# Rebuilding the first two batches of a fused attention and MLP kernel: loads by head pairs, global columns by one-hot matmuls, weights and MLP placed earlier

## The chip, the cores and the metric

The kernel runs on one core of one Trainium2 chip. The metric is the device time of one execution in microseconds (us); lower is better. A kernel's executions differ by about 1% among themselves, so a difference below about half a per cent is not a difference here.

The engines, as the profile names them: PE does matmuls (PEld its weight loads), DVE, ACT and POOL do elementwise work, SP issues DMAs. POOL and ACT issue DMAs too. SPq is SP's queue of issues. PEclk is the clock granted to PE, as a share of full speed.

## The reference, cut to what matters

Eight batches, eight heads, 576 tokens, head size 64 (model width 512). Attention sees a band of 32 tokens to either side and eight global tokens, which see and are seen by all. Then comes a ResMLP block: a mix over tokens, and an MLP over channels of width 2048.

```python
mask = np.abs(pos[:, None] - pos[None, :]) <= window            # 32
mask = mask | is_global[:, None] | is_global[None, :]
attn = softmax(where(mask, scale * q @ k.T, -1e9))
x = (attn @ v)                                                  # [8, 576, 512]
a1 = alpha1 * x + beta1
u = x + lam * np.einsum('ts,bsd->btd', w_tok, a1)               # token mixing
a2 = alpha2 * u + beta2
out = u + lam * (np.maximum(a2 @ w_ch1, 0.0) @ w_ch2)           # MLP
```

## The kernel before

The program is written as one order of instructions; each engine works off its own part of it in that order. Tokens of all batches are lined up and cut into nine groups of 512 for the MLP. Each group needs 64 matmuls with W1 and 64 with W2, 128x128 by 128x512, 1152 in all. They are the bulk of the work, and they are used as fill: the front of a batch (attention and token mixing) is a generator that yields how many MLP matmuls of earlier groups to put in.

```python
def filler():
    for g in range(9):
        while g >= done[0]:
            yield False
        yield from mlp(g)
fill = filler()
for _ in range(8):
    next(fill)
for b in range(1, NB):
    gen = front(b, kqn)
    ...                                  # for each n that gen yields: n times next(fill)
```

Within the front, batch b + 1 is prepared: K and Q arrive in five chunks, which POOL casts (`qk_chunk`), and which a transposing DMA then turns. Three small gathers fetch the K, Q and V rows of the global tokens. POOL also forms XL, the scaled attention output, from which token mixing reads. The V shift makes a second copy of V, offset by 64 tokens, with two DMAs. UT is the MLP's input, transposed.

```python
def front(b, kqn):
    x = pX.tile([P, 5, DM], FP32, name="x")
    if not last:
        cq = [qk_chunk(b + 1, c) for c in range(3)]      # loads on SP; casts later on POOL (G)
        kq, vg = gathers(b + 1)                          # three indirect DMAs on POOL
    yield from pg(b)
    yield from qk(b, 0)
    for c in range(2):
        if cq: cq.pop(0)(G)
    for p in range(4):                                   # head pairs
        ...                                              # scores of pair p + 1
        pv(b, p, x)                                      # P @ V, x on DVE, XL on POOL
        if not last:
            if p == 0:
                cq.pop(0)(G)
                cq = [qk_chunk(b + 1, c) for c in (3, 4)]
            elif p == 1:
                cq.pop(0)(G); cq.pop(0)(G)
            elif p == 2: ...                             # transposing DMAs of K and Q, loads of V
            else: ...                                    # casts of V, V shift, global V
        yield 2
    yield 22
    mix = tokmix(b, x)
    ...
```

The first two batches are written out by hand. In batch 0 all K and Q are loaded first, in halves of four heads. Batch 1's K and Q are loaded early, and cast and transposed between the steps of batch 0's attention and token mixing. Then V of batch 1, then W2:

```python
pv(0, 1, x)
drain(qk3)
xg(0, 2)
wt_tr(1)
kt(0, (SC, SC))                  # batch 1's K, pair 0: PE transposes, ACT copies
n_q0(SC)                         # batch 1's first Q half: cast on ACT
pv(0, 2, x)
w1_dma(0)
...
c_v = [v_part(1, i) for i in range(3)]
for c in c_v:
    c(G)                         # batch 1's V: casts on POOL
v_shift(G)
for blk in range(4):
    w2_dma(blk)                  # W2, four loads of 512 KB, issued by POOL
```

The softmax here doesn't subtract the row's maximum and nothing guards it: scores larger than these inputs give would overflow.

Of the kernel before, what the change touches and what calls it, by code (L numbers as in the profile page):

```python
# [20 lines left out]
D = 64  # L21
# [15 lines left out]
def _consts():  # L37
    p = np.arange(P)[:, None]
    t = np.arange(NSUB)[None, :]
    key = 64 * t - 32 + p  # L40
    q = np.arange(64)[None, :]
    band = ((p - q >= 0) & (p - q <= 2 * WIN)).astype(np.float32)
    valid = ((key >= 0) & (key < S)).astype(np.float32)
    h = (np.arange(P) % 64) // 8
    par = (h[:, None] % 2 == np.arange(2)[None, :]).astype(np.float32)
    bd = (h[:, None] == np.arange(8)[None, :]).astype(np.float32)
    oh = (np.arange(P)[:, None] % 8 == np.arange(8)[None, :]).astype(np.float32)
    hoff = ((h * S)[:, None] + np.arange(8)[None, :] * H * S).astype(np.float32)
    return np.concatenate([key.astype(np.float32), valid, band, par, bd, oh, hoff], axis=1).astype(np.float32)


C_KEY, C_VALID, C_BAND, C_PAR, C_BD, C_OH, C_HOFF = 0, 9, 18, 82, 84, 92, 100
C_W = 108
# [3 lines left out]
def kernel(  # L57
# [89 lines left out]
    b2a = cp.tile([P, 4], BF16, name="b2a")  # L147

    wt16 = A(HTb, 0, [[704, 5], [1, 704]])
    KQ0 = 3520  # L150
# [10 lines left out]
    def qk4_half(b, i, hh, r):  # L161
        nc.sync.dma_start(
            out=A(r, 0, [[256, 4], [1, 256]]),
            in_=(k, q)[i][b, 4 * hh : 4 * hh + 4, 0:512, :].rearrange("h (p c) d -> p h (c d)", c=4),
        )
        return lambda E: copy(E, out=A(HTb, KQ0 + 2560 * i + 256 * hh, [[64, 4], [512, 4], [1, D]]), in_=A(r, 0, [[256, 4], [64, 4], [1, D]]))

    def qk4_rest(b, r):
        for i, src in enumerate((k, q)):
            nc.sync.dma_start(out=A(r, 0, [[64, 8], [1, 64]], 64 * i, 64), in_=src[b, :, 512:576, :].rearrange("h p d -> p h d"))  # L170
        return lambda E: copy(E, out=A(HTb, KQ0 + 2048, [[1, 512]]), in_=r[:, 0:512])
# [34 lines left out]

    def v_shift(E):
        E.dma_start(out=A(vo, 0, [[1, 2080]], 0, 64), in_=A(ve, 0, [[1, 2080]], 64, 64))
        E.dma_start(out=A(vo, 0, [[1, 2080]], 64, 64), in_=A(ve, 520, [[1, 2080]], 0, 64))

    def gathers(b):
        kq = pS.tile([P, D], FP32, name="kq")
        vg = pS.tile([64, D], FP32, name="vg")
# [3 lines left out]
        G.indirect_dma_start(out=vg, out_offset=None, in_=vf, in_offset=off)  # L217
        return kq, vg
# [115 lines left out]
    def pv(b, p, x):  # L334
        par = b % 2
        ptz, gs, rs, xl = PTz[p % 2], GS[par], RS[par], XL[par]
        xps = psX.tile([P, 2, 512], FP32, name="xps")
        for hh in range(2):
            h = 2 * p + hh
            for u in range(5):  # L340
                o_ = xps[:, hh, 65 * u : 65 * u + 65]
# [6 lines left out]
                T.matmul(out=o_, lhsT=gs[:, P * u : P * u + P], rhs=rs[:, h, :], start=False, stop=True)  # L348
        rden = pS.tile([P, 2, 5], FP32, name="rden")
        V.tensor_scalar(out=rden, in0=A(xps, 64, [[512, 2], [65, 5]]), scalar1=EPS, scalar2=None, op0=ALU.add)  # L350
        V.reciprocal(out=rden, in_=rden)
        V.tensor_tensor(  # L352
            out=A(x, P * p, [[64, 2], [DM, 5], [1, 64]]),
            in0=A(xps, 0, [[512, 2], [65, 5], [1, 64]]),
            in1=A(rden, 0, [[5, 2], [1, 5], [0, 64]]),
            op=ALU.mult,
        )
        full, edge, r0 = (0, 4, 0) if par == 0 else (1, 0, 64)
        G.tensor_tensor(  # L359
# [5 lines left out]
        G.tensor_tensor(  # L365
# [43 lines left out]
    def front(b, kqn):  # L409
# [3 lines left out]
        if not last:  # L413
            cq = [qk_chunk(b + 1, c) for c in range(3)]
            kq, vg = gathers(b + 1)
# [5 lines left out]
        for p in range(4):  # L421
# [11 lines left out]
            if not last:  # L433
                if p == 0:
                    cq.pop(0)(G)
                    cq = [qk_chunk(b + 1, c) for c in (3, 4)]
                elif p == 1:
                    cq.pop(0)(G)
                    cq.pop(0)(G)
                elif p == 2:  # L440
# [5 lines left out]
                else:  # L446
# [5 lines left out]
        yield 22  # L452
# [46 lines left out]
    nc.sync.dma_start(out=gi_t, in_=bass.AP(gi32.tensor, gi32.offset, [[0, P], [1, 16]]))  # L499
    nc.sync.dma_start(out=cst, in_=nc.inline_tensor(_consts(), name="cst_np").ap())  # L500
    scr, a1b, b1r, colr = u_tile(), u_tile(), u_tile(), u_tile()
    stage = [pUT.tile([P, 1024], FP32, name="UT") for _ in range(2)]
    c_k0 = qk4_half(0, 0, 0, next_r())
    c_q0 = qk4_half(0, 1, 0, next_r())
    c_rest = qk4_rest(0, stage[1])
    c_k1 = qk4_half(0, 0, 1, next_r())
    c_q1 = qk4_half(0, 1, 1, stage[0])

    make_identity(nc, identb)
    G.memset(dum, 0.0)  # L510
    SC.activation(out=dum, in_=dum, func=AF.Exp)
    G.memset(RV[0][0:32, 0:512], 0.0)
    G.iota(colr, pattern=[[1, DM]], base=0, channel_multiplier=0, allow_small_or_imprecise_dtypes=True)
    G.memset(GS[0], 0.0)
    G.memset(RS[0], 0.0)
    G.memset(A(PTz[1], 0, [[128, 19], [1, 64]]), 0.0)

    V.memset(KTz, 0.0)
    V.memset(KgT, 0.0)
    V.memset(A(QT, 1664, [[80, 16], [1, 8]]), 0.0)  # L520
    V.memset(A(ve, 64, [[65, 40], [1, 1]]), 1.0)
    for t_ in GRT:
        V.memset(t_, 0.0)
    SC.copy(out=A(kz, 64, [[256, 20], [64, 2], [1, 64]]), in_=A(KTz, 0, [[128, 20], [64, 2], [1, 64]]))
    SC.copy(out=A(PTz[0], 0, [[128, 19], [1, 64]]), in_=A(KTz, 0, [[64, 19], [1, 64]]))
    V.tensor_copy(out=gbc, in_=A(gi_t, 0, [[2, 8]]))
    V.tensor_tensor(out=scr[:, 0:8], in0=gbc, in1=cst[:, C_OH : C_OH + 8], op=ALU.mult)
    V.tensor_reduce(out=gsel[:, 0:1], in_=scr[:, 0:8], axis=mybir.AxisListType.X, op=ALU.add)
    V.tensor_tensor(out=hg_idx, in0=cst[0:64, C_HOFF : C_HOFF + 8], in1=A(gsel, 0, [[0, 8]], 0, 64), op=ALU.add)
    kq, vg = gathers(0)  # L530
    masks_a(scr)

    def kt(p, engs):
        ps = ml(BF16)
        for c in range(4):
            T.transpose(out=ps[:, c * P : (c + 1) * P], in_=A(HTb, KQ0 + 512 * c + P * p, [[1, P]]), identity=identb)
        for hh in range(2):
            copy(engs[hh], out=A(KTz, 640 * (2 * p + hh) + 32, [[4, P], [1, 4]], 64 * hh, 64), in_=A(ps, 0, [[1, P], [P, 4]], 64 * hh, 64))

    def qt(p):  # L540
        ps = sc(BF16)
        for c in range(4):
            T.transpose(out=ps[:, c * P : (c + 1) * P], in_=A(HTb, KQ0 + 2560 + 512 * c + P * p, [[1, P]]), identity=identb)
        for e in range(2):
            SC.copy(out=A(QT, 1600 * e + 80 * p, [[320, 4], [4, 16], [1, 4]]), in_=A(ps, 16 * e, [[32, 4], [1, 16], [P, 4]]))  # L545

    def rest():
        ps = ml(BF16)
        for p in range(4):
            T.transpose(out=ps[:, P * p : P * p + P], in_=A(HTb, KQ0 + 2048 + P * p, [[1, P]]), identity=identb)  # L550
        for hh in range(2):
            V.tensor_copy(out=A(KTz, 640 * hh + 544, [[1280, 4], [1, 64]], 64 * hh, 64), in_=A(ps, 0, [[P, 4], [1, 64]], 64 * hh, 64))
        SC.copy(out=A(QT, qo(8), [[80, 4], [1, 64]]), in_=A(ps, 64, [[P, 4], [1, 64]]))

    c_k0(V)
    c_v = [v_part(0, i) for i in range(3)]
    nc.sync.dma_start(out=a1b, in_=moe_alpha1.unsqueeze(0).to_broadcast([P, DM]))
    nc.sync.dma_start(out=lamb, in_=moe_lam.unsqueeze(0).to_broadcast([P, DM]))
    for r0 in (0, 64):
        nc.sync.dma_start(out=b1r[r0 : r0 + 1, :], in_=moe_beta1.unsqueeze(0))  # L560
    nc.sync.dma_start(out=a2b, in_=moe_alpha2.unsqueeze(0).to_broadcast([P, DM]))
    with nc.allow_non_contiguous_dma(reason="column-major 512-vector load (one time)"):
        nc.sync.dma_start(out=b2c, in_=moe_beta2.rearrange("(c p) -> p c", p=P))
    kt(0, (V, V))
    c_q0(SC)
    qt(0)
    c_rest(V)
    rest()
    G.memset(ecol, 0.0)
    G.memset(A(ecol, 0, [[64, 2]]), 1.0)  # L570
    G.memset(wt16[:, :, 576:704], 0.0)
    G.memset(wt16[64:P, 4, :], 0.0)
    G.memset(ve[96:P, 4, :, 0:64], 0.0)
    c_k1(SC)
    kt(1, (V, V))
    qt(1)
    masks_b(scr)
    c_q1(SC)
    kt(2, (V, SC))
    qt(2)  # L580
    kqn = glob_kq(kq)
    kt(3, (V, SC))
    qt(3)
    glob(kqn)
    c_v[0](G)
    c_v[1](G)
    c_v[2](G)
    v_shift(nc.sync)
    for c in (0, 1):
        G.dma_start(  # L590
            out=(wt16[:, 0:4, 0:S], wt16[0:64, 4, 0:S])[c],
            in_=(moe_w_tok[0:512, :].rearrange("(c p) s -> p c s", p=P), moe_w_tok[512:576, :])[c],
        )
    V.tensor_scalar(out=gsel[:, 1:2], in0=gsel[:, 0:1], scalar1=-512.0, scalar2=None, op0=ALU.add)
    gs_init(0, colr)
    V.tensor_copy(out=A(RS[0], 64, [[65, 8]], 0, 64), in_=cst[0:64, C_BD : C_BD + 8])
    glob_v(V, 0, vg)
# [51 lines left out]
    for _ in range(3):  # L649
        next(qk2)  # L650
# [113 lines left out]
```

## Time and profile before

| before | |
|---|---|
| time | 424.12 us, median of 3 (421.89 to 424.3) |
| PE busy | 380.1 of 422.4 us (90%) |
| first attention matmul, batch 0 / batch 1 / batch 2 | 16.38 / 57.48 / 106.90 us |
| token mixing begins, batch 0 / batch 1 | 44.33 / 94.90 us |
| first MLP matmul / first W2 matmul / first matmul of group 1 | 55.75 / 77.92 / 111.86 us |

The page cuts the span into 40 slices of about 10.6 us. Digits are the busy share in tenths. PE has its idle time in the first twelve slices and is practically full afterwards: only the first two batches can give time.

```profile
PE   1657798959599999999999999999999999999995
PEclk9967999987699999999999999999999999999999
DMA  8994999999986999898999989979981003202001
GB/s 233 216 289 75 169 214 194 201 168 209 217 163 89 169 229 223 129 219 152 230 154 194 211 197 156 193 175 223 167 195 55 2 2 99 64 0 76 25 25 74
```

What PE waits for between 14 and 135 us (instruction, what released it, us in total, times, longest):

```profile
PE sc L392 <- POOL XL_116 L365: 4.9, 1, 4.9
PE ml L469 <- DMA UT<-u_1502: 4.3, 1, 4.3
PE xps L347 <- DMA vo<-ve: 2.7, 2, 2.3
```

These are batch 1's token mixing waiting for POOL's last product, the MLP's group 1 waiting for its transposed input, and P @ V waiting for the V shift (2.3 us of it in batch 0). POOL's order in batch 1, from its timeline (start, duration, engine, line, output<-input, and in brackets the idle time before it and what ended it):

```profile
59.14 1.04 POOL L110 CAST ve<-RV_99 128x1024 f16<-128x1024 f32 x1 [11.42 <-PE ml L469]
62.23 3.05 POOL L633 DMA_DIRECT2D W_119<-in_moe_w_ch_dram  x4
68.14 0.90 POOL L217 DMA_INDIRECT vg<-in_v_dram,hg_idx  x1 [0.30 <-issue]
81.72 0.62 POOL L110 CAST q_101<-R_95 128x512 bf16<-128x512 f32 x1 [5.91 <-DMA R_95<-in_q_dram]
83.65 0.46 POOL L365 TENSOR_TENSOR XL_116<-x,LA_133 64x128 bf16<-64x128 f32 x1
94.40 0.45 POOL L365 TENSOR_TENSOR XL_116<-x,LA_133 64x128 bf16<-64x128 f32 x1
```

W2 is issued at 62.23, the last gather of batch 2 at 68.14. POOL stands 5.91 us for a chunk of Q, and its last XL product, at 94.40, releases token mixing.

### The profile page before, as it was taken

Reading aid. Unit: us, or ns where it says so; the run is one execution under the profiler, and the core shown is the slowest. Engines: PE = TensorE matmul, PEld = TensorE weight load, DVE = VectorE, ACT = ScalarE, POOL = GpSimd, SP = SyncE. Lnnn points to the kernel's source line nnn. Section 1 sums busy time; section 2 is a strip of 40 time slices with the busy share of each in tenths; the row PEclk is TensorE's granted clock in tenths of the full one; section 3 lists DMA queues with packets and bytes.
Section 4 is the critical chain, followed back from the end, with each engine's and each line's share of the span. In section 5 each row is a group of like instructions: output and inputs, shape, how many; then the busy total and the mean of one; then the engine's idle time right before and its main releaser. Section 6 shows DMA issues by size and latency. Waiting matters only on the chain.

```text
span 422.4 us, 8398 instructions
## 1 busy us (share of the span) xinstructions
PE 380.1 (90%) x3347; PEld 212.0 (50%) x3403; DVE 229.9 (54%) x454; ACT 172.7 (41%) x303; POOL 181.4 (43%) x241
## 2 busy tenths in 40 slices
PE   1657798959599999999999999999999999999995
PEld 1556355624266456645654565456545654444442
DVE  6946655627435674668558653966474547204022
ACT  6738546400185027503740474037404730450720
POOL 7647536393435465645573565637440330000000
PEclk9967999987699999999999999999999999999999
DMA  8994999999986999898999989979981003202001
GB/s 233 216 289 75 169 214 194 201 168 209 217 163 89 169 229 223 129 219 152 230 154 194 211 197 156 193 175 223 167 195 55 2 2 99 64 0 76 25 25 74
DMA packets 174282, 64.14 MB, mean 152 GB/s; under 512 B 158498, under 2 KB 168226, under 8 KB 174244
## 3 DMA queue, kind: packets, MB, share of 16 engines
q1 hardware_dynamic: 167524, 54.63, 63.5%
q0 software_dynamic: 6720, 8.98, 12.0%
q8 instruction: 26, 0.43, 0.4%
q14 instruction: 12, 0.10, 0.1%
HBM read 39.28 MB, written 9.44 MB: 115 GB/s over the span
## 4 chain that ended last, share of the span: by engine, by line
PE 66%; DMA 10%; DVE 8%; POOL 6%; issue 4%; SPq 4%; ACT 1%; POOLq 0%; DVEq 0%
PE ml L469 24%; PE ml L478 23%; PE sc L392 7%; DMA vg<-in_v_dram,hg_idx 3%; PE sc L285 3%; PE xps L347 3%; DMA HTb<-in_moe_w_tok_dram 2%; DMA RV_99<-in_v_dram 2%; DVE U L393 2%; PE xps L348 2%; SPq L203 2%; PE mm L313 2%; POOL XL_116 L359 1%; PE sc L330 1%; DVE tmp L483 1%
## 5 line engine op out<-in xcount | busy, mean ns | idle before, releaser
L469 PE MATMUL ml<-UT,W_118 128*128 128x512 bf16 x540 | 140.6, 383 | 6.6 <-DMA UT<-u_1502 4.3
L478 PE MATMUL ml<-W_119,HTb 128*128 128x512 bf16 x559 | 135.4, 381 | 0.8
L472 ACT ACTIVATE HTb<-ml,bias1T 128x512 bf16<-128x512 f32 x144 | 98.9, 688 | 87.6 <-PE ml L469 75.0
L478 PEld LDWEIGHTS <-HTb 128*128 128x128 bf16 x576 | 54.8, 98 | 60.1 <-issue 1.1
L469 PEld LDWEIGHTS <-W_118 128*128 128x128 bf16 x576 | 49.3, 99 | 45.4 <-issue 6.2
L483 DVE TENSOR_TENSOR tmp<-ml,lamb 128x512 f32<-128x512 f32 x36 | 24.9, 690 | 69.7 <-PE ml L478 67.4
L292 ACT ACTIVATE Pt<-sc 128x432 f16<-128x432 f32 x90 | 47.4, 528 | 13.9 <-PE sc L285 13.7
L285 PEld LDWEIGHTS <-KTz 128*128 128x128 bf16 x576 | 31.5, 103 | 21.5 <-PE mm L232 1.1
L393 DVE TENSOR_TENSOR U<-sc,x 128x512 f32<-128x512 f32 (+1 forms) x40 | 27.4, 685 | 26.2 <-PE sc L392 26.1
L359 POOL TENSOR_TENSOR XL_116<-x,LA_133 128x512 bf16<-128x512 f32 x16 | 20.3, 1267 | 35.1 <-DVE x L352 35.1
L285 PE MATMUL sc<-QT,KTz 128*128 128x72 bf16 x540 | 33.1, 200 | 1.1 <-ACT QT L545 1.1
L359 POOL TENSOR_TENSOR XL_115<-x,LA_133 128x512 bf16<-128x512 f32 x16 | 21.4, 1337 | 26.1 <-DVE x L352 26.1
L392 PE MATMUL sc<-XL_116,wtT_122 128*128 128x512 bf16 x99 | 26.2, 395 | 5.0 <-POOL XL_116 L365 4.9
L331 ACT ACTIVATE GS_110<-sc 64x320 f16<-64x320 f32 (+1 forms) x8 | 3.2, 405 | 60.8 <-PE sc L330 60.5
L484 DVE TENSOR_TENSOR U<-tmp,U 128x512 f32<-128x512 f32 x36 | 27.3, 758 | 1.2
L352 DVE TENSOR_TENSOR x<-xps,rden 128x640 f32<-128x640 f32 x32 | 26.4, 825 | 1.6
L392 PE MATMUL sc<-XL_115,wtT_121 128*128 128x512 bf16 x98 | 24.4, 379 | 0.4 <-DVE U L393 0.2
L331 ACT ACTIVATE GS_111<-sc 64x320 f16<-64x320 f32 (+1 forms) x8 | 3.2, 403 | 52.3 <-PE sc L330 52.3
L110 POOL CAST ve<-RV_98 128x1024 f16<-128x1024 f32 x8 | 9.2, 1155 | 31.5 <-DMA RV_98<-in_v_dram 31.4
L347 PEld LDWEIGHTS <-PTz_106 128*128 128x128 f16 x288 | 16.2, 102 | 6.6 <-DMA vo<-ve 2.9
L294 DVE TENSOR_TENSOR GRT_108<-Pt,grm 128x80 f16<-128x80 f16 x16 | 5.2, 324 | 26.4 <-ACT Pt L292 26.4
L348 PE MATMUL xps<-RS_112,GS_110 128*128 128x65 f16 x160 | 17.2, 203 | 2.4 <-DVE RS_112 L321 2.4
(185 smaller groups left out, 524.4 us busy)
## 6 DMA issues: line engine op xcount, KB each, us to landing
out_dram<-U SPq DMA_DIRECT2D x36, 256.0 KB, 2.9
RV_99<-in_v_dram SPq DMA_DIRECT2D x16, 256.0 KB, 4.9
vo<-ve POOLq DMA_DIRECT2D x14, 260.0 KB, 3.9
R_97<-in_k_dram SPq DMA_DIRECT2D x12, 256.0 KB, 4.3
R_97<-in_q_dram SPq DMA_DIRECT2D x12, 256.0 KB, 5.5
RV_98<-in_v_dram SPq DMA_DIRECT2D x8, 256.0 KB, 3.7
W_118<-in_moe_w_ch_dram POOLq DMA_DIRECT2D x4, 512.0 KB, 8.9
W_119<-in_moe_w_ch_dram POOLq DMA_DIRECT2D x4, 512.0 KB, 11.6
```

The lines of the kernel that those rows point to most:

```text
L285: T.matmul(out=ps[:, i * 144 + 72 * hh : i * 144 + 72 * hh + 72], lhsT=KTz[:, 2 * p + hh, 64 * t : 64 * t + P], rhs=A(QT, qo(t) + 80 * p, ...
L292: SC.activation(out=Pt[:, 432 * un : 432 * un + 432], in_=ps[:, 0:432], func=AF.Exp, bias=0.0, scale=0.125)
L347: T.matmul(out=o_, lhsT=ptz[:, base : base + P], rhs=vv, start=(i == 0), stop=False)
L352: V.tensor_tensor(out=A(x, P * p, [[64, 2], [DM, 5], [1, 64]]), in0=A(xps, 0, [[512, 2], [65, 5], [1, 64]]), in1=A(rden, 0, [[5, 2], [1, 5 ...
L359: G.tensor_tensor(out=A(xl, DM * full + P * p, [[DM, 4], [1, P]]), in0=A(x, DM * full + P * p, [[DM, 4], [1, P]]), in1=A(LA1, P * p, [[0, ...
L392: T.matmul(out=ps, lhsT=wtT[par][:, c, P * u : P * u + P], rhs=XL[par][:, c, :], start=(c == 0), stop=(c == 4))
L393: V.tensor_tensor(out=U[f][r0:r1, :], in0=ps[r0:r1, :], in1=x[r0:r1, u, :], op=ALU.add)
L469: T.matmul(out=ps, lhsT=W1[:, cc, ec * P : (ec + 1) * P], rhs=ut[:, cc, :], start=(cc == 0), stop=(cc == 3))
L472: SC.activation(out=HTb[:, slots[ec], :], in_=ps, func=AF.Relu, bias=bias1T[:, ec : ec + 1], scale=1.0)
L478: T.matmul(out=ps, lhsT=HTb[:, slots[ec], P * j : P * j + P], rhs=W2[:, ec, :], start=(ec == 0), stop=(ec == 15))
L483: V.tensor_tensor(out=tmp, in0=ps, in1=lamb, op=ALU.mult)
L484: V.tensor_tensor(out=u, in0=tmp, in1=u, op=ALU.add)
```

## The change

Its intent: start batch 0's attention sooner (small loads by head pairs, no V shift through DMA, global columns picked out of K and Q by matmuls with one-hot columns instead of gathers), bring W1 ahead of batch 1's K and Q, and begin the MLP before batch 1's attention, so that PE has fill earlier.

In outline. Batch 0: K and Q in pairs of heads, V in two halves of the heads, the V shift as copies on DVE, global K and Q columns by `kq_glob`. W1 before batch 1's loads:

```diff
-    c_k0 = qk4_half(0, 0, 0, next_r())
-    ... (all of batch 0's K and Q in halves of four heads)
+    c_k01 = kq_load(nc.sync, 0, 0, 0, 2, R[0], 0)
+    c_q01 = kq_load(nc.sync, 0, 1, 0, 2, stage[0], 0)
+    ... (heads 2 and 3, then V's first half, heads 4 to 7, V's second half)
+def kq_glob(p):
+    ps = mm()
+    for i in range(2):
+        for c in range(4):
+            T.matmul(out=ps[:, 8 * i : 8 * i + 8], lhsT=kq4(i, p, c), rhs=onehot[:, c, :], start=(c == 0), stop=False)
+        T.matmul(out=ps[:, 8 * i : 8 * i + 8], lhsT=A(kz, 2048 + P * p, [[1, P]]), rhs=onehot[:, 4 + i, :], start=False, stop=True)
+    ... (two DVE copies)
-    v_shift(nc.sync)
+    vo_half(V, 0)
...
+    w1_dma(2)
+    w1_dma(3)
+    pv_norm(0, 2, x, m2, V)
+    pv_norm(0, 3, x, m3, V)
+    n_k0 = kq_load(G, 1, 0, 0, 4, R[0], 0)          # batch 1, issued by POOL
+    n_q0 = kq_load(G, 1, 1, 0, 4, R[1], 0)
+    n_rest = kq_rest(G, 1, u_tile())
+    n_k1 = kq_load(G, 1, 0, 4, 4, R[2], 0)
+    n_q1 = kq_load(G, 1, 1, 4, 4, RV[1], 0)         # in a buffer that batch 1's V needs next
```

Batch 1 is now prepared after batch 0's token mixing, beside the first 44 MLP matmuls, with its casts on DVE:

```diff
+    fillers(20)
+    for p in range(4):
+        if p % 2 == 0:
+            (n_k0, n_k1)[p // 2](V)
+        kt(p, (V, V))
+        if p % 2 == 0:
+            (n_q0, n_q1)[p // 2](V)
+        if p == 2:
+            c_v += [v_part(1, i) for i in (1, 2)]   # loads of V into RV[1] and R
+        if p == 0:
+            n_rest(V)
+            V.memset(RV[0][64:65, 0:1], 0.0)
+            c_v = [v_part(1, 0)]
+        fillers(3)
+        qt(p, (V, SC))
+        fillers(3)
+        ...
+        kq_glob(p)
+    c_v[0](G)
+    c_v[1](G)
+    w2_dma(0)
+    c_v[2](G)
+    v_shift(G)
+    for blk in range(1, 4):
+        w2_dma(blk)
```

In batch 1's front the chunk casts of batch 2 come one head pair later, and some fills are held back for the wait at the MLP's group 1:

```diff
-            cq = [qk_chunk(b + 1, c) for c in range(3)]
+            if b > 1:
+                cq = [qk_chunk(b + 1, c) for c in range(3)]
...
-                if p == 0:
+                late = b == 1
+                if p == late:
+                    if late:
+                        cq = [qk_chunk(b + 1, c) for c in range(3)]
+                        cq.pop(0)(G)
+                        cq.pop(0)(G)
                     cq.pop(0)(G)
                     cq = [qk_chunk(b + 1, c) for c in (3, 4)]
-                elif p == 1:
+                elif p == 1 + late:
...
-        yield 22
+        yield 10 if b == 1 else 22
...
-            for _ in range(n):
-                next(fill)
+            fillers(n if b > 1 or used[0] < 64 or n > 3 else 0)
```

## The prediction

> **What bounds the kernel now.** The page shows PE busy 90% of a 422.4 us span: 380.1 us of matmul, 42 us idle. Busy time by stretches puts nearly all idle time early: PE is busy 1.3, 6.7, 5.5, 8.0, 7.6 and 8.0 us of the first six tens, 5.1 and 7.6 us at 90-110, and about 99% from 130 to 400. The granted clock is 0.72 and 0.60 at 20-40, 0.66 at 90-100 and at 110-120. The Trainium skill ("TensorE: Matmul & The Clock Gate", the HAM clock gate) says that idle windows halve the clock; this trace agrees: token-mix matmuls after the 4.9 us wait at 90 start about 0.42 us apart, later ones 0.216. The steady state is matmul-bound; only the first two batches can give time.
>
> The chain of waits and the timeline show there:
> - Attention starts at 16.4 us, behind all K/Q loads, then waits for the V shift copies (until 25.6) and for the token weights (landed 29.2).
> - DMA moves 47 GB/s at 35-40: W1 is issued at 40-46, because POOL stands behind the XL products. The MLP starts at 55.8, batch 1's attention at 57.6 with only 8 of 1152 MLP matmuls done.
> - In batch 1 POOL casts batch 2's chunks ahead of its XL products; a q chunk landed behind W2 at 81.7, token mixing waits until 94.9 (4.9 us). At 106.9-111.9 PE waits for the transposed UT, group 0's 128 matmuls being used up.
>
> **What the change does.** It removes batch 0's two V shift DMAs and two batches' K/Q gathers; loads by head pair put the first attention matmul near 10 us. Added: 80 one-hot matmuls of 8 columns (estimate 2-4 us of PE, largely in idle time), some copies on DVE. Moved: W1 ahead of batch 1's K/Q; 44 MLP matmuls before batch 1's attention; batch 2's chunk casts one pair later; 11 matmuls of group 0 kept back to cover the UT transposes.
>
> **Costing (estimates from traced durations).** W1 or W2 takes about 15 us of DMA, a batch's K/Q in 1 KB pieces 7.5, V 5.3. Without the 35-45 hole, batch 1's K/Q land near 50. DVE then needs about 12 us of casts and copies, which the 24 matmuls between them overlap. Batch 1's attention starts near 60, no earlier than before, but with 36 more matmuls done (36 x 0.216 = 7.8 us). W2 and batch 2's chunks share the DMA until about 80; batch 1's token mixing starts near 88-90, and batch 2's attention near 100 instead of 112, with 11 matmuls (2.4 us) more still to do. Net 9-11 us, plus 1-2 us of cold clock, all on the critical path, since PE is full afterwards.
>
> **Prediction: 411 us, 8 in 10 between 402 and 419.** Faster by over 2%: 0.72; within 2%: 0.26; slower: 0.02.
>
> **What would show it.** First attention matmul at 9-11 us; no DMA hole at 35-45; MLP begun before 50; batch 1's attention at 57-62; wait before its token mixing under 4 us; UT wait gone; PE about 99% after 110. PE busy nearly unchanged, less idle time.
>
> **What would make it wrong.** POOL casts more first, so the token weights are issued at 21-24 rather than 18.3: perhaps a new DMA hole. If DMA volume, not order, sets batch 2's start (the Trainium skill, "DMA: Bandwidth & Descriptors", "Issuing engines are not separate DMA queues": all share 16 engines; the busy share of 0.9-1.2 at 40-110 fits), the gain shrinks to about 4 us. If W2 lands late, PE idles in batch 1 and the clock drops again. If all waits vanish, about 402.

## The result, and the profile after

The kernel after takes 441.18 us (median of 4, 440.52 to 443.75), beside 424.21 us before (median of 4): 1.0421 of before, 95% interval 1.0364 to 1.0479. It is slower by about 17 us. (All ratios here are the mean time of one kernel's runs over that of the other's of the same rounds, so not quite the ratio of the medians.) Executions over 1.5% slower than the fastest of the same kernel are left out of the means. The result is correct. The clock is not the reason: its mean in the profiled run is 0.977, against 0.965 before. PE is idle for 51.7 us of the span (438.8 less 387.1 busy), before for 42.3. (Before's trace lacks the records of 53 of the 1152 MLP matmuls, so its busy time is somewhat too low.)

| event, us | before | predicted | after |
|---|---|---|---|
| first attention matmul, batch 0 | 16.38 | 9 to 11 | 13.25 |
| token mixing, batch 0 | 44.33 | | 44.65 |
| first MLP matmul | 55.75 | before 50 | 53.60 |
| batch 1's attention | 57.48 | 57 to 62 | 71.92 |
| first load of W2 issued | 62.23 | | 75.10 |
| token mixing, batch 1 | 94.90 | 88 to 90 | 109.85 |
| batch 2's attention | 106.90 | near 100 | 121.89 |
| first matmul of group 1 | 111.86 | | 130.51 |

The lead of 3.1 us at the start is gone at batch 0's token mixing, batch 1's attention is 14.4 us late, and at group 1 the kernel is 18.65 us behind. At the end it is 16.4 us behind (438.8 against 422.4).

```profile
PE   1675878492959999999999999999999999999995
PEclk9999999889788999999999999999999999999999
DMA  8967948978999798999998897969994002301001
GB/s 161 243 94 107 271 105 145 195 117 150 168 199 220 141 186 201 203 139 207 210 203 158 189 236 139 173 175 236 147 176 121 25 4 72 84 2 70 27 24 72
```

In the third slice (21 to 32 us) DMA moves 94 GB/s instead of 289. The hole at 35 to 40 us that the change was to close is still there in part (107 in the fourth slice, 75 before), and a new one opens between 55 and 77 us (105 and 145 GB/s in the sixth and seventh slices, 214 and 194 before). PE's waits of 14 to 135 us:

```profile
PE sc L443 <- POOL XL_116 L416: 6.9, 1, 6.9
PE ml L526 <- DMA UT<-u_1614: 4.5, 1, 4.5
PE ml L535 <- DMA W_119<-in_moe_w_ch_dram: 4.1, 1, 4.1
PE sc L598 <- DVE kz L113: 2.7, 2, 1.6
```

The first two are those of before, 2.0 and 0.2 us longer; the wait for W2 (W_119) is new. POOL's timeline tells why:

```profile
66.15 1.04 POOL L113 CAST ve<-RV_98 128x1024 f16<-128x1024 f32 x1 [16.07 <-DVE kz L113]
73.31 1.85 POOL L113 CAST ve<-RV_99 128x1024 f16<-128x1024 f32 x1 [6.13 <-DMA RV_99<-in_v_dram]
75.10 0.79 POOL L564 DMA_DIRECT2D W_119<-in_moe_w_ch_dram  x1
77.50 2.34 POOL L564 DMA_DIRECT2D W_119<-in_moe_w_ch_dram  x3
83.00 0.90 POOL L238 DMA_INDIRECT vg<-in_v_dram,hg_idx  x1 [0.64 <-DMA W_119<-in_moe_w_ch_dram]
89.42 1.26 POOL L410 TENSOR_TENSOR XL_116<-x,LA_133 128x512 bf16<-128x512 f32 x1 [5.52 <-DVE x L403]
96.02 0.61 POOL L416 TENSOR_TENSOR XL_116<-x,LA_133 64x128 bf16<-64x128 f32 x1 [5.35 <-DMA vg<-in_v_dram,hg_idx]
105.49 0.61 POOL L113 CAST q_101<-R_96 128x512 bf16<-128x512 f32 x1 [0.35 <-DMA R_96<-in_q_dram]
109.35 0.45 POOL L416 TENSOR_TENSOR XL_116<-x,LA_133 64x128 bf16<-64x128 f32 x1
```

Read it downwards. The cast of RV_99 waits 6.13 us for its data. SP issues that load only when the buffer is free, and the buffer holds batch 1's second Q half until DVE has cast it, at 67.93:

```profile
57.70 0.68 DVE L113 CAST kz<-R_95 128x1024 bf16<-128x1024 f32 x1
67.93 0.69 DVE L113 CAST kz<-RV_99 128x1024 bf16<-128x1024 f32 x1
```

```profile
68.65 1.00 SPq L209 DMA_DIRECT2D RV_99<-in_v_dram  x2
99.56 0.37 SPq L184 DMA_DIRECT2D R_96<-in_k_dram  x1
101.59 0.61 SPq L184 DMA_DIRECT2D R_97<-in_q_dram  x1
```

In the timeline POOL works off its instructions in the program's order, so W2 stands behind that cast and is issued at 75.10, 13 us later than before, and the gathers behind W2. Then POOL waits 5.35 us, until 96.02, for the last gather, before an XL product that in the source does not use it (the built program makes this product wait for the three gathers). Only then come the chunk casts, which set the buffers free for the last chunks, so that these are issued at 99.56 to 101.59 and cast from 104.5 on. The last XL product is at 109.35.

### The profile page after: what moved, and what is told of

Read it like the earlier page. It is cut to its first block, busy times and chain, and to the rows that moved or that the text cites. A ratio compares the mean times of both kernels' runs of the same rounds, so it can differ in the third digit from the quotient of the medians.

```text
span 438.8 us, 8684 instructions
## 1 busy us (share of the span) xinstructions
PE 387.1 (88%) x3496; PEld 214.0 (49%) x3496; DVE 239.8 (55%) x491; ACT 162.6 (37%) x288; POOL 184.2 (42%) x245
## 4 chain that ended last, share of the span: by engine, by line
PE 71%; DMA 12%; DVE 9%; issue 2%; POOL 2%; ACT 1%; ACTq 0%; SPq 0%; POOLq 0%; DVEq 0%
PE ml L526 27%; PE ml L535 24%; PE sc L443 7%; PE sc L313 3%; PE xps L382 3%; DMA vg<-in_v_dram,hg_idx 3%; PE mm L341 2%; DMA R_97<-in_q_dram 2%; PE xps L383 2%; DMA W_119<-in_moe_w_ch_dram 2%; DVE U L444 2%; PE sc L358 1%; DMA R_96<-in_q_dram 1%; DMA UT<-u_1564 1%; DVE KTz L113 1%
## 5 line engine op out<-in xcount | busy, mean ns | idle before, releaser
L526 PE MATMUL ml<-UT,W_118 128*128 128x512 bf16 x576 | 145.0, 383 | 5.0 <-DMA UT<-u_1614 4.5
L535 PE MATMUL ml<-W_119,HTb 128*128 128x512 bf16 x576 | 140.7, 383 | 4.1 <-DMA W_119<-in_moe_w_ch_dram 4.1
L526 PEld LDWEIGHTS <-W_118 128*128 128x128 bf16 x576 | 49.9, 99 | 48.2 <-issue 6.5
L410 POOL TENSOR_TENSOR XL_116<-x,LA_133 128x512 bf16<-128x512 f32 x16 | 20.3, 1268 | 42.3 <-DVE x L403 42.2
L113 POOL CAST ve<-RV_98 128x1024 f16<-128x1024 f32 (+1 forms) x9 | 9.5, 1058 | 54.7 <-DMA RV_98<-in_v_dram 38.6
L410 POOL TENSOR_TENSOR XL_115<-x,LA_133 128x512 bf16<-128x512 f32 x14 | 18.8, 1342 | 17.8 <-DVE x L403 15.2
L403 DVE TENSOR_TENSOR x<-xps,rden 128x640 f32<-128x640 f32 x30 | 24.7, 825 | 1.4
L443 PEld LDWEIGHTS <-wtT_122 128*128 128x128 bf16 x100 | 10.1, 101 | 20.0 <-issue 9.1
```

Source lines behind the costliest of these rows:

```text
L410: E.tensor_tensor(out=A(xl, DM * full + P * p, [[DM, 4], [1, P]]), in0=A(x, DM * full + P * p, [[DM, 4], [1, P]]), in1=A(LA1, P * p, [[0, ...
L443: T.matmul(out=ps, lhsT=wtT[par][:, c, P * u : P * u + P], rhs=XL[par][:, c, :], start=(c == 0), stop=(c == 4))
L526: T.matmul(out=ps, lhsT=W1[:, cc, ec * P : (ec + 1) * P], rhs=ut[:, cc, :], start=(cc == 0), stop=(cc == 3))
L535: T.matmul(out=ps, lhsT=HTb[:, slots[ec], P * j : P * j + P], rhs=W2[:, ec, :], start=(ec == 0), stop=(ec == 15))
```

## The experiments

Theory A says that POOL's order makes the loss: W2 and the gathers stand behind V casts that wait. Theory B: the later place of the chunk casts delays the last chunk loads. Rivals: C, the fills that are held back starve PE; D, DVE's load delays batch 1's attention and all else follows; E, W1 and batch 1's loads are still issued too late. In the tables, the times of events (in us) are from the profiled run; group 1 is the first matmul of the MLP's second group. DVE's "13.6 of 15 us" in some of the expectations adds up durations that overlap; the window 57.6 to 72.6 shows 12.09 us busy.

### W2 first, buffers, chunks, fills: one at a time

`w2_early` moves W2's loads to about 50 us, ahead of batch 1's preparation:

```diff
     G.tensor_tensor(out=XL[1][0:1, 0, :], ...)
+    for blk in range(4):
+        w2_dma(blk)
...
     c_v[1](G)
-    w2_dma(0)
     c_v[2](G)
     v_shift(G)
-    for blk in range(1, 4):
-        w2_dma(blk)
```

> The changed kernel, with the four W2 loads issued on POOL before batch 1's head pairs (at 50-57 us) and no longer behind the casts of batch 1's V (75-80 us). Theory A (the loss comes from W2 and the gathers queued on POOL behind V's casts): the 4.1 us wait for W2 and the 5.4 us POOL wait for the gathers go, batch 1's token mixing starts at 95-99 us, not 109.9; time 424-430 us. Theory B (the later chunk casts are the cause): token mixing still starts after 105 us; time above 436.

`v1_own_buffer` gives batch 1's second Q half a buffer that V does not need, so V can be loaded at once:

```diff
-    n_q1 = kq_load(G, 1, 1, 4, 4, RV[1], 0)
+    n_q1 = kq_load(G, 1, 1, 4, 4, pUT.tile([P, 1024], FP32, name="UT"), 0)
...                                     # and all three v_part(1, i) at p == 0
```

> The changed kernel, with batch 1's second Q half loaded into a free UT buffer instead of RV_99, so that all of V of batch 1 is loaded after the first head pair (61-64 us) rather than after the third (68.7). Theory A: V lands by 67, W2's first block is issued at 67 instead of 75.1, and everything after moves up by 6-8 us; time 432-435 us. Theory B or D (DVE work of batch 0 and 1 as the cause): within 2 us of 441.

`chunks_as_before` undoes the later place of the chunk loads and casts:

```diff
-            if b > 1:
-                cq = [qk_chunk(b + 1, c) for c in range(3)]
+            cq = [qk_chunk(b + 1, c) for c in range(3)]
-                late = b == 1
+                late = 0
```

> The changed kernel, with batch 2's chunk loads and casts at the head pairs where the kernel before has them (undoes 'late'). Theory A: it helps only as far as the last two chunks are loaded earlier (before 95 instead of 99.6-105.5): token mixing at 101-106 instead of 109.9; time 434-438 us. Theory B: most of the loss returns; time below 430.

`fill_as_before` undoes the holding back of fills:

```diff
-        yield 10 if b == 1 else 22
+        yield 22
-            fillers(n if b > 1 or used[0] < 64 or n > 3 else 0)
+            fillers(n)
```

> The changed kernel, with the MLP matmuls handed out in batch 1 as in the kernel before (22 ahead of token mixing, none held back). Theory A and B: PE waits for data in batch 1 in both, so 47 more matmuls only move waits about; the wait for W2 gets longer; within 3 us of 441. Theory C (the holding back starves PE): time below 434.

| run | median us | of before | 95% interval | batch 1 attention | batch 1 token mixing | group 1 |
|---|---|---|---|---|---|---|
| after | 441.18 | 1.0421 | 1.0364 to 1.0479 | 71.92 | 109.85 | 130.51 |
| w2_early | 435.08 | 1.0254 | 1.0194 to 1.0314 | 74.20 | 104.90 | 125.12 |
| v1_own_buffer | 436.35 | 1.0292 | 1.0233 to 1.0352 | 71.76 | 104.86 | 125.36 |
| chunks_as_before | 434.02 | 1.0219 | 1.0156 to 1.0282 | 72.09 | 107.68 | 125.54 |
| fill_as_before | 447.26 | 1.0558 | 1.0478 to 1.0637 | 71.86 | 112.81 | 133.99 |

(The kernel before had a median of 424.5 us in the rounds of the last four, its slow run included.)

A and B each get back a part, about 7 and 9 us (1.0421 less 1.0254 and less 1.0219, times 424); w2_early had been expected to give more. v1_own_buffer shortens the same chain as w2_early, though less than expected (W2 issued at 70.43, not 67), and gets back about 5 us. In chunks_as_before POOL still waits for the gather (6.11 us, until 96.59), as A has it. C falls: with the fills let go the kernel is 6 us slower, where A and B, too, had expected a change of at most 3. The fills are used up early, and PE then stands for group 1's input:

```profile
133.99 1.44 PE L526 MATMUL ml<-UT,W 128*128 128x512 bf16 x3 [11.77 <-DMA UT<-u]
```

### Both orders at once, and the rivals

`w2_early_chunks` is w2_early and chunks_as_before together.

> Both w2_early and chunks_as_before in one kernel. They took 6.1 and 7.2 us off the changed kernel alone. If they cure two links of one chain (POOL's order in batch 1), the sum holds or more: token mixing of batch 1 at 95-98 us, where PE alone would get to it; time 425-430 us. If each merely uncovers the same next wait, the two together stay near one: above 432.

`casts_on_pool` tests D: batch 1's K and Q casts move from DVE to POOL, and one of each two copies of the K transposes to ACT, with the order otherwise as in after.

```diff
-            (n_k0, n_k1)[p // 2](V)
-        kt(p, (V, V))
+            (n_k0, n_k1)[p // 2](G)
+        kt(p, (V, SC))
...                                     # n_q0, n_q1 and n_rest on G as well
```

> The changed kernel, with the five casts of batch 1's K and Q on POOL (idle at 50-66 us) and half of the key copies on ACT, as the kernel before has them. Theory D (DVE, busy 13.6 of the 15 us at 57.6-72.6, holds batch 1's attention): it starts at 65-67 us instead of 71.9, RV_99 comes free by 62, W2 is issued at 65-67; time 428-433 us. If PE or the loads set the pace there: start after 70, within 2 us of 441.

`w1_ahead_of_xl` tests E: the last two loads of W1 and batch 1's first K and Q loads are issued right behind W1's second load.

```diff
     w1_dma(1)
+    w1_dma(2)
+    w1_dma(3)
+    n_k0 = kq_load(G, 1, 0, 0, 4, R[0], 0)
+    n_q0 = kq_load(G, 1, 1, 0, 4, R[1], 0)
     vo_half(V, 1)
...                                     # and not at their old places
```

> The changed kernel, with W1's last two blocks and half of batch 1's K/Q issued on POOL ahead of the XL products (at 31-34 us instead of 39-42). The prediction had counted on the DMA hole at 35-40 closing, and it did not. If batch 1's start waits for its K/Q, it gains up to 7 us; by theory D the casts wait for DVE, not for the loads (K of the first half has landed by about 51, the cast starts at 57.7), so the loads come 6-7 us earlier and the time falls by under 2 us.

`w2_chunks_pool` is w2_early_chunks and casts_on_pool together.

> w2_early, chunks_as_before and casts_on_pool in one. If the three are separate parts of the loss: batch 1's attention at 65-67 us, its token mixing at 90-93; 418-424 us, level with the kernel before or just better. If batch 2's loads (DMA volume) set the start of batch 2, no gain over w2_early_chunks.

| run | median us | of before | 95% interval | batch 1 attention | batch 1 token mixing | group 1 |
|---|---|---|---|---|---|---|
| w2_early_chunks | 426.29 | 0.9991 | 0.9938 to 1.0043 | 73.49 | 104.28 | 118.14 |
| casts_on_pool | 436.0 | 1.0239 | 1.0181 to 1.0297 | 67.25 | 103.03 | 124.54 |
| w1_ahead_of_xl | 441.35 | 1.0367 | 1.0303 to 1.0432 | 71.70 | 109.66 | 130.22 |
| w2_chunks_pool | 427.39 | 1.0017 | 0.9966 to 1.0069 | 73.60 | 104.74 | 119.03 |

(Before: 426.49 us in these rounds.)

The two orders together take off the whole slowdown, so A and B are its cause. In w2_early_chunks no XL product of batch 1 waits for a gather, and PE works without a gap into token mixing:

```profile
50.15 1.56 POOL L563 DMA_DIRECT2D W<-in_moe_w_ch_dram  x2
88.61 0.46 POOL L416 TENSOR_TENSOR XL<-x,LA 64x128 bf16<-64x128 f32 x1
103.78 0.45 POOL L416 TENSOR_TENSOR XL<-x,LA 64x128 bf16<-64x128 f32 x1
```

```profile
104.28 1.24 PE L443 MATMUL sc<-XL,wtT 128*128 128x512 bf16 x5
```

It does not run as before does, though. Batch 1's token mixing comes at 104.28 (95 to 98 had been expected; 94.90 before) and batch 2's attention at 114.05 (106.90 before). From there to batch 3's attention it needs 40.0 us and before 46.0, of which 4.3 us are the wait at group 1: the fills held back make up for most of the late start.

E falls: W1 and K come earlier (DMA moves 142 GB/s at 20 to 40 us instead of 101), and nothing that follows moves. D is not shown to be a cause of its own. casts_on_pool has batch 1's attention 4.7 us earlier and gets back about 8 us (1.0421 less 1.0239), more than that lead; but with the casts done earlier the buffer RV_99 comes free earlier too, and W2 goes out at 67.21 instead of 75.10:

```profile
67.21 0.79 POOL L564 DMA_DIRECT2D W<-in_moe_w_ch_dram  x1
```

That is A's chain again, and this run can't separate the two. On top of the two orders the same casts give nothing (w2_chunks_pool), and there batch 1's attention starts at 73.60, not at the 65 to 67 expected. In w2_chunks_pool other DVE work runs beside POOL's casts: four DVE instructions that take 1.31 us in after take 4.93.

```profile
54.32 4.93 DVE L287 TENSOR_SCALAR GS<-U,gsel 8x512 f16<-8x512 f32 x4
```

### V ahead, casts on ACT, fills again, V shift on ACT

`v1_first` starts from chunks_as_before, gives the second Q half its own buffer, and issues V's loads ahead of the 20 matmuls; W2's place in the order is that of after. `v1_first_act` adds K's casts on ACT (and one of each two K copies). `v1_first_act_fill` adds fill_as_before to that. `vo_on_act` is after, with the V shift copies of batch 0 on ACT.

```diff
+    c_v = [v_part(1, i) for i in (0, 1)]            # v1_first
     fillers(20)
     for p in range(4):
         if p % 2 == 0:
-            (n_k0, n_k1)[p // 2](V)
+            (n_k0, n_k1)[p // 2](SC)                # v1_first_act
-        kt(p, (V, V))
+        kt(p, (V, SC))                              # v1_first_act
```

```diff
-    vo_half(V, 0)
+    vo_half(SC, 0)                                  # vo_on_act; and vo_half(SC, 1)
```

> chunks_as_before, and batch 1's V put ahead of W2 in time and not only in POOL's order: the second Q half goes to a free UT buffer, V's first two parts are loaded at about 47 us. Theory A: V is cast by 56-58, W2's first block is issued at 56-58 and the rest at 62-64, the V shift lands before 75, and batch 1 waits for neither W2 nor the shift. It keeps what w2_early_chunks gained (426.3) and takes 2-5 us more: 421-425 us, just under the kernel before. If the K/Q loads, now sharing the DMA with V, delay batch 1's attention (over 74 us instead of 72), it gains nothing over w2_early_chunks.

> v1_first, with K's two casts of batch 1 and half of the key copies on ACT instead of DVE (about 4.2 us less on DVE in the pair loop). Theory D for the late start of batch 1's attention (DVE, busy 13.6 of 15 us there): it starts at 67-69 us instead of 72, and the time falls by 3-4 us below v1_first. If PE's own transposes and MLP matmuls set the pace: within 1 us of v1_first.

> v1_first_act, with the MLP matmuls handed out in batch 1 as in the kernel before. With W2 landed in time they have data, so they fill PE's gaps in batch 1 (PE was busy 13.2 of 20 us at 80-100 in w2_early_chunks), unlike in fill_as_before, which lost 6 us; but group 0 is then used up before the UT transposes land, which costs 3-5 us of wait again. Between -4 and +2 us against v1_first_act.

> The changed kernel, with the V shift copies of batch 0 on ACT (busy 7.1 of the 20 us at 20-40) instead of DVE (busy 17.6). Token mixing of batch 0 starts at 44.65 in the changed kernel and at 44.33 in the one before, although its attention starts 3.1 us earlier. If DVE is what holds it (theory D), 1.8 us of copies off DVE move it to 43-43.5, and the time falls by up to 1.5 us; if the token weights or W1 hold it, no change.

| run | median us | of before | 95% interval | batch 1 attention | batch 1 token mixing | group 1 |
|---|---|---|---|---|---|---|
| v1_first | 427.52 | 1.0075 | 1.0018 to 1.0132 | 72.87 | 99.17 | 119.17 |
| v1_first_act | 424.73 | 1.0036 | 0.998 to 1.0091 | 73.86 | 101.03 | 116.26 |
| v1_first_act_fill | 436.18 | 1.0298 | 1.0238 to 1.0358 | 75.10 | 105.17 | 122.45 |
| vo_on_act | 443.37 | 1.0484 | 1.0415 to 1.0552 | 73.26 | 111.89 | 131.70 |

(Before: 423.96 us in these rounds.)

v1_first is a second way to the same end, without touching W2's line: V's data are there early, POOL is not held, W2 goes out at 65.68, and 1.0219 of chunks_as_before becomes 1.0075. It supports A from the other side, but missed its own figures (W2 at 56 to 58, 421 to 425 us), and its interval still lies above 1. v1_first_act missed as well: batch 1's attention starts at 73.86 and not at 67 to 69, and its gain on v1_first is within the noise. v1_first_act_fill costs 11 us more than v1_first_act, where 2 us at most had been expected, again with a wait for group 1's input (9.83 us at 122.45): the change was right to hold fills back. vo_on_act missed: it is no faster than after, since ACT, too, worked in the program's order. The copies there took 2.14 us and stood ahead of batch 0's exponentials, so that PE waited 1.60 us and batch 0's token mixing began at 46.26 instead of 44.65.

```profile
25.01 2.14 ACT L113 COPY vo<-ve 64x1040 f16<-64x1040 f16 x2
27.18 0.70 ACT L359 ACTIVATE GS<-sc 64x320 f16<-64x320 f32 x2
27.66 0.52 PE L313 MATMUL sc<-QT,KTz 128*128 128x72 bf16 x6 [1.60 <-ACT GS L359]
```

### Where the predicted gain goes

With the orders put right the kernel only equals the one before. The predicted gain of 9 to 13 us was still missing, so six more runs follow the lead through the program. All start from v1_first_act; `base_again` is that kernel once more, in the same rounds.

> The same kernel as v1_first_act, again, as the base of the three beside it: 1.0036 of before in its first rounds, so within 0.5 per cent of before here.

`casts_ahead` takes batch 1's casts from behind the MLP's bias copies and its first 20 matmuls:

```diff
+    n_k0(SC)
+    n_q0(V)
     fillers(20)
     for p in range(4):
-        if p % 2 == 0:
-            (n_k0, n_k1)[p // 2](SC)
         kt(p, (V, SC))
-        if p % 2 == 0:
-            (n_q0, n_q1)[p // 2](V)
+        if p == 1:
+            n_k1(SC)
+            n_q1(V)
```

> v1_first_act, with the casts of batch 1's first K and Q halves placed ahead of the first 20 MLP matmuls, and those of the second halves during the second head pair. If the late casts hold back batch 1's attention, PE's waits for them (1.71, 0.73 and 2.13 us at 60 to 68) go, the attention starts near 69 to 70 instead of 73.9, and the whole takes 3 to 4 us less than base_again. If the lead is lost again later (PE then waits for DVE and POOL before batch 1's token mixing), the attention starts early too, but the whole changes by less than 1.5 us.

`kt_on_act` takes load off DVE in batch 0: `kt(2, (SC, SC))` and `kt(3, (SC, SC))` in place of `(V, SC)`. `ahead_kt_act` does both.

> v1_first_act, with both copies of batch 0's third and fourth K transposes on ACT instead of one on DVE. If DVE's queue eats batch 0's lead, PE's wait of 1.98 us at 22.32 shrinks to under 1 us, token mixing of batch 0 starts 1 to 2 us earlier than 44.8, and the whole takes 1 to 2 us less than base_again. If POOL's casts of V (until about 25) are what comes last, token mixing starts within 0.5 us of where it did and the whole stays.

> Both changes at once. If both leads are kept, 4 to 6 us less than base_again, so near 0.99 of before, the first version under it. If one is eaten later, no less than the better of the two alone.

casts_ahead's trace then led to the last two. `gathers_early` is casts_ahead with batch 2's gathers issued at 50 us; `gathers_w2_early` issues half of W2 right behind them.

```diff
     G.tensor_tensor(out=XL[1][0:1, 0, :], ...)
+    early = [gathers(2)]
+    w2_dma(0)                                       # gathers_w2_early only; and w2_dma(1)
...
-            kq, vg = gathers(b + 1)
+            kq, vg = early.pop() if early else gathers(b + 1)
```

> casts_ahead, with the three gathers of batch 2 issued on POOL at about 50 us, ahead of batch 1's pair loop and of W2's loads, instead of behind them at 70 to 75. If the gathers hold POOL, its wait of 5.79 us before the first edge product goes, PE's wait of 4.95 us before token mixing shrinks to under 2 us, token mixing of batch 1 starts near 94 to 95 instead of 98.0, and the whole takes 3 to 4 us less than casts_ahead: near 0.99 of before. If something else eats the lead (batch 2's loads, or the U buffers that wait for the MLP's output), token mixing starts earlier but batch 2's attention stays near 110 and the whole stays within 1 us.

> gathers_early, with the first two of W2's four loads issued right behind these gathers, at about 54 us, instead of among the V casts at 65. If W2's landing comes last next, PE's waits for it (0.36 us or more at 80 to 90) go and the whole takes another 1 to 2 us less. If V's and batch 2's loads share the DMA with it, those land later and it is no less, or 1 to 2 us more.

| run | median us | of before | 95% interval | batch 1 attention | batch 1 token mixing | batch 2 attention | group 1 |
|---|---|---|---|---|---|---|---|
| base_again | 425.38 | 1.0004 | 0.9977 to 1.0032 | 74.40 | 101.63 | 111.39 | 116.51 |
| casts_ahead | 425.79 | 1.0011 | 0.9985 to 1.0037 | 68.98 | 98.04 | 110.29 | 115.67 |
| kt_on_act | 424.91 | 0.9985 | 0.9964 to 1.0007 | 74.70 | 100.96 | 110.72 | 116.30 |
| ahead_kt_act | 426.05 | 1.0010 | 0.9983 to 1.0036 | 69.05 | 100.33 | 111.77 | 117.88 |
| gathers_early | 424.71 | 0.9987 | 0.9946 to 1.0027 | 69.22 | 99.30 | 111.87 | 117.64 |
| gathers_w2_early | 423.98 | 0.9979 | 0.9941 to 1.0016 | 69.07 | 100.69 | 110.45 | 115.51 |

(Before: 425.46 us in the rounds of the first four, 425.27 in those of the last two.)

Not one of the six differs from before by more than the noise, and the expectations of several microseconds all missed. They show where the lead goes, though. casts_ahead has batch 1's attention 5.4 us earlier than base_again, token mixing 3.6, batch 2's attention 1.1, and the whole is not faster. POOL eats the first part:

```profile
87.02 0.45 POOL L416 TENSOR_TENSOR XL<-x,LA 64x128 bf16<-64x128 f32 x1 [5.79 <-DMA vg<-in_v_dram,hg_idx]
97.54 0.45 POOL L416 TENSOR_TENSOR XL<-x,LA 64x128 bf16<-64x128 f32 x1
```

```profile
98.04 0.59 PE L443 MATMUL sc<-XL,wtT 128*128 128x512 bf16 x1 [4.95 <-POOL XL L416]
```

It waits for batch 2's gathers, which are issued behind W2, and from 87.02 to 98.0 works without a gap. gathers_early takes that wait away, as expected, and another stands in its place at once, the data of batch 2's chunks:

```profile
80.92 0.61 POOL L113 CAST q<-R 128x512 bf16<-128x512 f32 x1 [7.78 <-DMA R<-in_q_dram]
87.58 0.61 POOL L113 CAST kz<-R 128x512 bf16<-128x512 f32 x1 [4.29 <-DMA R<-in_k_dram]
```

```profile
99.30 0.58 PE L443 MATMUL sc<-XL,wtT 128*128 128x512 bf16 x1 [3.75 <-POOL XL L416]
```

Those chunks share the DMA with W2. With half of W2 earlier (gathers_w2_early), V comes later instead: POOL's last big V cast is at 69.37 instead of 64.56, and PE waits 3.08 us for the V shift at 80.78. The Trainium skill ("DMA: Bandwidth & Descriptors", "Issuing engines are not separate DMA queues") says that DMAs from all issuing engines run on the same 16 DMA engines and interleave. The last two runs agree: with the DMA's busy share at 1.06 to 1.10 from 40 to 80 us in both, the transfer that was brought forward (W2) pushed another back (V, by 4.8 us).

That there is so much left to move after 40 us is the change's own doing. The two stretches of 20 to 40 us, with before's first and gathers_early's second (columns: stretch, length, busy us of PE, PEld, DVE, ACT, POOL with instruction counts, clock, DMA busy share, GB/s):

```profile
20.00:40.00 20.00, 13.50 (x219) 12.24 (x218) 10.41 (x27) 10.60 (x21) 12.03 (x15) 0.66 0.84 200
```

```profile
20.00:40.00 20.00, 13.46 (x225) 11.32 (x223) 17.23 (x48) 6.90 (x16) 16.63 (x21) 1.00 0.59 102
```

Before used that time to load batch 1's K and Q and the token weights at 200 GB/s. The new order leaves DMA half used there (102 GB/s): POOL is busy (16.63 of 20 us, with V's casts until 25.2 and then XL products), and half of W1 and batch 1's loads stand behind that, until 39.42 and later. That is about 2 MB (98 GB/s times 20 us) which must be moved later, when V, W2 and batch 2's chunks want the DMA too. Part of it is made up at once: at 40 to 60 us gathers_early moves 230 GB/s and before 169. Counted from 0 us (207 and 228 GB/s in the first 20), it is about 1.2 MB behind at 60 us; at its 190 GB/s of 60 to 80 us that is an estimated 6 us, about half of the predicted gain. This last step is argued from the windows, not shown by a run: w1_ahead_of_xl filled a part of the hole, but with POOL's later order unmended, so it could not tell. No version that fills the hole and has the later order right was run.

kt_on_act answers for the other suspect. PE's wait at 22 us fell from 1.98 to only 1.46 us, and batch 0's token mixing began at 44.00 instead of 44.18: relieving DVE by this much is worth next to nothing, since another DVE instruction then makes PE wait (2.19 us at 28.27).

## Why the prediction was wrong

- **What bounds the kernel: right.** PE is practically full after 140 us in both kernels, and the whole difference is made before 131 us.
- **First attention matmul at 9 to 11 us: too early.** It was 13.25, 3.1 us earlier than before. The chain to it runs through the load of the last 64 tokens' K and Q, 256-byte runs, 8.56 us from issue to landing at about 11.0.
- **"DVE then needs about 12 us of casts and copies" and "Batch 1's attention starts near 60": wrong.** The term was not badly sized: from the first K cast at 57.70 to the last DVE instruction of the loop at 72.4 it is 14.7 us. It was put in the wrong place. The casts stand behind token mixing and the bias copies of 20 matmuls, not at the landing of K. Before, this preparation ran inside batch 0's attention. The 36 early MLP matmuls (an estimated 7.8 us) are less than the 14.4 us by which batch 1's attention is late.
- **"W2 and batch 2's chunks share the DMA until about 80; batch 1's token mixing starts near 88-90": the step that failed.** It costed volume, and took each transfer to be issued as soon as DMA had room. W2 was issued at 75.10, because POOL's queue stood behind a V cast, whose load stood behind a buffer, which a DVE cast held. The gathers and chunk casts came behind W2. Token mixing began at 109.85. Undoing the two orders took the whole 4.2% back (w2_early_chunks, 0.9991); that is shown. Even then token mixing began at 104.28, not 88 to 90, so the predicted start of batch 2 was not reached in any run (earliest 110.29, in casts_ahead).
- **"If W2 lands late, PE idles in batch 1 and the clock drops again": named as a danger, and right,** but given 2 in 100 with the whole slowdown. PE waited 4.10 us for W2 at 82.78. The clock: the Trainium skill ("TensorE: Matmul & The Clock Gate", "The HAM clock gate") says that an idle window halves it. The traces agree: in after the first five token-mix matmuls after a wait of 6.94 us take 2.29 us, and five later ones, at 116.01, take 1.24 us.
- **The UT wait gone: wrong** in after (4.53 us). Where the order is mended it does go (none of 0.5 us or more in w2_early_chunks), thanks to the fills held back. That part of the change does what it was meant to.
- **"The gain shrinks to about 4 us" if DMA volume sets the pace:** nothing of it is left, and no run separates volume from order in that. The lead of 3.1 us at the first attention was gone at batch 0's token mixing (44.65 against 44.33), with DVE busy 17.64 of 20 us at 20 to 40 us (10.41 before), and later leads went to waits of POOL and for DMAs, as the traces of the last runs show.

What stays open: whether any order of this design beats before. Of the versions run, none does beyond the noise; the lowest ratio is 0.9979 (0.9941 to 1.0016).

## What to carry to other kernels

Cost a moved load by where its issue stands in its engine's queue and by what frees its buffer, not only by its bytes: follow each instruction ahead of it to what that one waits for. When one wait has been taken away, look for the next one before counting the gain: here the lead of 5 us met the gathers, then the chunk loads, then the V shift. And ask of a new order which engine or DMA it leaves idle early, since that work comes back later, at a busier time (argued here from the windows, not shown by a run).

## What the Trainium skill lacked or had wrong

- "DMA: Bandwidth & Descriptors", "Issuing engines are not separate DMA queues": it says that issuing from several engines saves only the sequencer's time to start a DMA, usually small. That section does not say that an issue also waits for all that stands ahead of it in its engine's order. Here the issue itself took 0.79 us, but W2 was issued 13 us later than before because it stood behind a V cast on POOL, and an earlier place in the same queue was worth about 7 us of the whole (1.0421 to 1.0254). No run moved W2 to another engine's queue.
- The same page, "Two DMAs through the same engine are not ordered", says that descriptors within one queue of one DMA engine start in order. It gives no figure for a small indirect gather behind large loads. Here three gathers issued at 80.14 to 83.00, behind 2 MB of W2 in POOL's queue, had landed only by 96.0; in gathers_early, issued at 50.41 to 53.54 ahead of W2, no instruction was found waiting for them.
- "SBUF — State Buffer", "Who interferes with whom", says that DVE and GpSimd can block each other for a whole instruction. It gives two slowdown factors, but not for instructions this small. The traces agree in direction: a DVE instruction on 128x9 elements took 2.15 us beside a cast and a memset of POOL, and 0.17 us in before, and the four shown above 4.93 instead of 1.31. That the lock is the reason was not tested.
